# One tile or three for the column pieces of w_in

## The chip, the cores and the metric

The kernel runs on one core of a Trainium2 chip, in one launch. The metric is the time of an execution on the device in microseconds (us); lower is better. Five engines of the core matter: TensorE (PE; its weight loads are listed apart as PEld), VectorE (DVE), ScalarE (ACT), GpSimd (POOL) and SyncE (SP). Each works through its own list of instructions in order and waits on semaphores for what other engines or transfers (DMAs) must have done first. SP issues the loads of q, k, v and f_logit and the stores of the output; POOL issues the loads of the two weight matrices, among its other work.

## The reference

Two computations stand one behind the other: a recurrence over the sequence with a gate per element, and a two-layer feed-forward block on its output.

```python
B, H, S, D = q.shape                       # 4, 8, 768, 48
f = 1.0 / (1.0 + np.exp(-f_logit))
for t in range(S):
    state = f[:, :, t, :, None] * state + np.einsum('bhd,bhe->bhde', k[:, :, t], v[:, :, t])
    y[:, :, t] = np.einsum('bhd,bhde->bhe', q[:, :, t], state)
...
x = np.ascontiguousarray(y.transpose(0, 2, 1, 3)).reshape(B * S, H * D)     # 3072 x 384
h = x @ w_in                               # w_in: 384 x 2048
g = np.maximum(0.01 * h, h)
return (g @ w_out).astype(np.float32)      # w_out: 2048 x 384
```

## The kernel before

**Chunks and pairs.** The sequence is cut into 6 chunks of 128 steps. Inside a chunk the recurrence is done with matmuls on all 128 steps at once; between chunks a state is carried. The 4 batch rows go two by two, so there are 12 pairs j of (chunk, half of the batch); in a pair, a = 0 or 1 names the batch row. One (j, a) is a unit of 128 tokens.

**The order is written out by hand.** A long string `order` lists steps such as `uu_0_0_1`, and a loop at the end of the function records them one by one. Each engine runs its share in this order. The first number is j, the second as a rule a. The steps that matter here:

- `Lf`, `Lk`, `Lq`, `Lv` (line 98): SP loads 192 KB of one input for one unit. Each input has six buffers.
- `gate` (lines 136 and 137, ACT), `cs` (142 and 145, PE), `dec` (152 to 156, ACT): the gate's logarithm, its running sum by a matmul with a triangle, and the factors from it. `k` (161) and `q` (167) scale k and q, on DVE for early pairs and on POOL for later ones; `v` (174 and 175, POOL) casts v into two layouts.
- `tk`, `tq` (188, PE) and `ck`, `cq` (191, DVE): transposes. `sc` (207, PE): scores of a unit into tile pw; `mk` (212, DVE): the mask; `mx` (240, PE): the mix of values into py; `xt` (246, DVE): py becomes xT, the transposed tokens that the feed-forward block reads. `pt` (251, PE), `sf` (256 and 257, DVE), `sb` (261 and 264, POOL): the state.
- `uu_j_a_g` (line 289, PE): a quarter g of the up-projection of one unit, 12 matmuls: four blocks ff = 4g to 4g + 3 of 128 of the 2048 columns, three steps kk of 128 of the 384 rows. `pu` (294, ACT): the leaky ReLU of that quarter. `up` (276) and `pr` (282) are the same for both units of later pairs, two blocks at a time. Tile pm has two buffers, so PE fills one while ACT empties the other.
- `dn_j_a_quarter` (299, PE): four matmuls of the down-projection; `ob` (304, DVE) takes the result out of PSUM, `st` (312, SP) stores it. The last unit has its own steps, `dp`, `op` and `sp` (321, 327, 332).
- `W_piece_...` (function `weights`): POOL issues the transfer of a piece of the weights, which come as float32 and are written as bfloat16. Before the first, a copy of one number makes POOL wait for the load that the step names (line 108). Pieces 0 to 2 are columns 0 to 511, 512 to 1023 and 1024 to 2047 of w_in (line 111); pieces 3 to 6 are quarters of w_out (line 115).
- `H_piece` (function `hold`, line 128): SP issues a transfer of four numbers out of a piece of the weights, and so waits until that piece has landed; the loads behind it on SP wait with it. The order uses `H_4` alone, the second quarter of w_out.

**The weights on the chip.** w_in lies in one tile, `w_in_b` of shape [128, 3, 2048]: in each of the 128 partitions three rows kk of 2048 numbers one behind the other. Which columns make up a block ff is told by `columns(ff)`: with c, a = divmod(ff, 4), every fourth column from 512c + a on, within the 512 columns of group c. So quarter g of a unit reads the columns 512g to 512g + 511: quarter 0 those of the first piece, quarter 1 those of the second, quarters 2 and 3 those of the third.

**Around the pieces, in the order.** `W_0`, `W_1`, `W_2` and `W_3` are recorded among the steps of pairs 0 and 1. On PE, what reads w_in first is `uu_0_0_0` and `uu_0_1_0`; then come `sc_1_1`, `mx_1_0`, `uu_0_0_1`, `uu_0_1_1`, `pt_1_0`, `uu_1_0_0`, `mx_1_1`, `uu_1_0_1`, `uu_0_0_2`, `uu_0_1_2`, `pt_1_1`, `uu_0_1_3`, `uu_0_0_3`, and the first step of the down-projection, `dn_0_0_0`. The waits are not written by hand: the framework derives them from which parts of which tiles an instruction reads or writes.

Of the kernel before, what the change touches and what calls it, by code (L numbers as in the profile page):

```python
# [10 lines left out]
BF16 = mybir.dt.bfloat16  # L11
# [4 lines left out]
def kernel(  # L16
# [10 lines left out]
    nc = tc.nc  # L27
# [6 lines left out]
    KD, FF = moe_w_in.shape  # L34
    NK, NF = KD // 128, FF // 128
# [8 lines left out]
    const = ctx.enter_context(tc.tile_pool(name="const", bufs=1))  # L44
# [29 lines left out]
    nc.gpsimd.memset(ones_col, 1.0)  # L74
    gate_w = const.tile([1, 8], FP32, tag="gate_w")

    w_in_b = const.tile([128, NK, FF], BF16, tag="w_in")
    w_out_b = const.tile([128, NF, KD], BF16, tag="w_out")

    for t in v2s:  # L80
# [4 lines left out]
    st = {j: {} for j in range(NP)}  # L85
# [7 lines left out]
    def raw(j, name):  # L93
        return once(j, name + "_raw", lambda: inp.tile([128, 2, H, D], FP32, name=f"{name}_raw", tag=f"{name}_raw"))
# [4 lines left out]
                          in_=srcs[name][2 * h + a, :, c * C:(c + 1) * C, :].rearrange("h t d -> t h d"))  # L99

    seen = set()
    w_in_cols = ((0, FF // 4), (FF // 4, FF // 2), (FF // 2, FF))

    def weights(piece, x, j, a):

        if (x, j, a) not in seen:
            seen.add((x, j, a))
            nc.gpsimd.tensor_copy(out=gate_w[:, 0:1], in_=raw(j, "fkqv"[x])[0:1, a, H - 1, D - 1:D])
        if piece < 3:
            lo, hi = w_in_cols[piece]  # L110
            nc.gpsimd.dma_start(out=w_in_b[:, :, lo:hi], in_=moe_w_in[:, lo:hi].rearrange("(k p) n -> p k n", p=128))  # L111
        else:
            n = NF // 4
            part = piece - 3
            nc.gpsimd.dma_start(
                out=w_out_b[:, part * n:(part + 1) * n, :],
                in_=moe_w_out[part * n * 128:(part + 1) * n * 128, :].rearrange("(p a) n -> p a n", a=n))
# [3 lines left out]
    def hold(piece):  # L121

        if piece < 3:
            hi = w_in_cols[piece][1]
            src = w_in_b[0:1, NK - 1, hi - 4:hi]
        else:
            src = w_out_b[0:1, (piece - 2) * (NF // 4) - 1, 0:4]
        nc.sync.dma_start(out=gate_s[:, 0:4], in_=src)
# [134 lines left out]
            rows = slice(64 * i, 64 * i + 64)  # L263
            nc.gpsimd.tensor_copy(out=sb[rows, a, :, i * D:i * D + D], in_=sf[rows, a])  # L264

    def columns(ff):

        c, a = divmod(ff, 4)
        return slice(512 * c + a, 512 * c + 512, 4)

    def up(j, g):
        pm = st[j]["pm", g] = ps_m.tile([128, 2, 256], FP32, name="pm", tag="pm")
        for i in range(2):
            ff = 2 * g + i
            for kk in range(NK):
                nc.tensor.matmul(pm[:, i, :], w_in_b[:, kk, columns(ff)],  # L276
                                 st[j]["xT"][:, kk].rearrange("t a s -> t (a s)"),
                                 start=(kk == 0), stop=(kk == NK - 1))

# [4 lines left out]
    def up_unit(j, a, g):  # L284
        pm = st[j]["pu", a, g] = ps_m.tile([128, 4, 128], FP32, name="pm", tag="pm")
        for i in range(4):
            ff = 4 * g + i
            for kk in range(NK):
                nc.tensor.matmul(pm[:, i, :], w_in_b[:, kk, columns(ff)], st[j]["xT"][:, kk, a, :],  # L289
                                 start=(kk == 0), stop=(kk == NK - 1))  # L290

    def relu_unit(j, a, g):
# [36 lines left out]
    def store_part(j, a, i):  # L329
# [8 lines left out]
        "xk": lambda j: turn_dma(j, "k"), "xq": lambda j: turn_dma(j, "q"),  # L338
        "sc": score, "mk": mask, "mx": mix, "xt": x_out, "pt": state, "sf": state_add, "sb": state_end,
        "up": up, "pr": relu, "uu": up_unit, "pu": relu_unit, "W": weights, "H": hold, "dn": down, "ob": out_copy, "st": store,  # L340
        "dp": down_part, "op": out_part, "sp": store_part,
        "Lf": lambda j, a: load(j, "f", a), "Lk": lambda j, a: load(j, "k", a),
# [96 lines left out]
```

## Time and profile before

| | |
|---|---|
| three runs | 194.6, 195.93 and 196.33 us, median 195.93 |
| the profiled execution | 195.9 us in all, span of the profile 194.1 us |
| PE busy | 173.9 us, 90% of the span |
| PEld, DVE, ACT, POOL busy | 71%, 50%, 51%, 39% |
| granted TensorE clock | 1.00 of full speed |
| transfers | 27.10 MB, 140 GB/s in the mean |
| w_in | two transfers of 384 KB and one of 768 KB, issued by POOL from 14.2 us on |

Times in the profile are counted from the start of the span. A row of the timeline gives the start, the length, the engine, line and operation, the tiles (out<-in), how many instructions are taken together, and in brackets for how long the engine had been idle before and what ended that. The chain of waits goes back from the last instruction to what released each step, and so holds only work that set the end. SPq and POOLq are the issuing of transfers; a transfer's time to landing counts from its issue. PE's matmuls overlap, so a group's length divided by its count is the pace, while the mean length of one is longer than that.

### The profile page before, as it was taken

The numbers are of one execution on the slowest core, as the hardware profiler recorded it, in microseconds if no ns is written. First come the engines' busy times: TensorE is split into PE (matmuls) and PEld (weight loads), VectorE is DVE, ScalarE is ACT, GpSimd is POOL, SyncE is SP. The second block draws the span as 40 slices with busy tenths as digits, with TensorE's granted clock in tenths as the row PEclk, the third lists the DMA queues.
The fourth block names the chain that finished last, engine by engine and source line by source line (L and its number), as shares of the span: only waits on it lengthen the run. The fifth ranks groups of instructions, "written<-read, shape, count | busy, mean of one in ns | idle before, by whom it ended". The sixth has DMA issues, their size and how long they took to land.

```text
span 194.1 us, 5638 instructions
## 1 busy us (share of the span) xinstructions
PE 173.9 (90%) x2360; PEld 138.1 (71%) x2360; DVE 97.5 (50%) x212; ACT 98.8 (51%) x201; POOL 75.1 (39%) x138
## 2 busy tenths in 40 slices
PE   0476229999999999999999999999999999999994
PEld 0343128977687888878888778877868888888663
DVE  2398503107688856966347737509737574200131
ACT  4544004726654788544976376974233544644200
POOL 8237060030439089401999373099653040000000
PEclk9999999999999999999999999999999999999999
DMA  6999999934999889979798989991001000021122
GB/s 121 210 197 169 204 195 206 173 75 111 200 213 206 191 160 230 178 171 211 162 239 195 210 184 212 194 244 57 26 19 57 28 5 3 3 78 44 41 81 81
DMA packets 106113, 27.10 MB, mean 140 GB/s; under 512 B 100456, under 2 KB 105192, under 8 KB 106088
## 3 DMA queue, kind: packets, MB, share of 16 engines
q1 hardware_dynamic: 104312, 23.60, 57.1%
q0 software_dynamic: 1776, 3.15, 9.0%
q8 instruction: 18, 0.29, 0.6%
q14 instruction: 7, 0.06, 0.1%
HBM read 25.17 MB, written 4.72 MB: 154 GB/s over the span
## 4 chain that ended last, share of the span: by engine, by line
PE 84%; DMA 8%; SPq 5%; POOL 1%; issue 0%; DVE 0%
PE po L299 31%; PE pm L276 22%; PE pm L289 12%; DMA w_in_b<-in_moe_w_in_dram 6%; PE py L240 5%; PE tp L188 5%; SPq L98 5%; PE pw L207 3%; PE cs L142 2%; DMA v_raw<-in_v_dram 2%; PE pt L251 2%; PE po L321 1%; POOL w_in_b L111 1%; PE cs L145 1%; DVE osb L327 0%
## 5 line engine op out<-in xcount | busy, mean ns | idle before, releaser
L299 PE MATMUL po<-w_out_b,gT 128*128 128x384 bf16 x368 | 71.4, 326 | 0.0
L282 ACT ACTIVATE gT<-pm 128x512 bf16<-128x512 f32 x64 | 37.9, 598 | 38.2 <-PE pm L276 37.5
L276 PE MATMUL pm<-xT,w_in_b 128*128 128x256 bf16 x384 | 51.5, 273 | 0.0
L299 PEld LDWEIGHTS <-gT 128*128 128x128 bf16 x368 | 34.1, 98 | 16.2 <-issue 0.2
L276 PEld LDWEIGHTS <-w_in_b 128*128 128x128 bf16 x384 | 40.7, 114 | 4.6
L212 DVE TENSOR_TENSOR wm<-pw,ut 128x512 bf16<-128x512 f32 x48 | 30.5, 683 | 14.8 <-PE pw L207 14.6
L289 PE MATMUL pm<-xT,w_in_b 128*128 128x128 bf16 x384 | 27.2, 225 | 7.0 <-DMA w_in_b<-in_moe_w_in_dram 7.0
L304 DVE COPY osb<-po 128x384 f32<-128x384 f32 x23 | 12.6, 553 | 37.8 <-PE po L299 36.5
L294 ACT ACTIVATE gT<-pm 128x512 bf16<-128x512 f32 x32 | 18.7, 596 | 24.8 <-PE pm L289 24.5
L289 PEld LDWEIGHTS <-w_in_b 128*128 128x128 bf16 x384 | 24.5, 116 | 9.3 <-issue 6.8
L167 POOL TENSOR_TENSOR qh<-q_raw,a_t 128x384 bf16<-128x384 f32 (+1 forms) x12 | 15.7, 1308 | 23.3 <-ACT a_end L156 15.8
L174 POOL CAST v_b<-v_raw 128x384 bf16<-128x384 f32 (+1 forms) x18 | 11.3, 625 | 33.1 <-DMA v_raw<-in_v_dram 32.3
L246 DVE CAST xT<-py 128x384 bf16<-128x384 f32 x24 | 12.7, 553 | 16.9 <-PE py L240 16.8
L152 ACT ACTIVATE em_t<-cs 128x384 bf16<-128x384 f32 x24 | 11.7, 488 | 12.3 <-PE cs L145 8.7
L261 POOL TENSOR_TENSOR sf<-sf,a_end 128x192 f32<-128x192 f32 x20 | 10.5, 523 | 18.9 <-DVE sf L257 18.6
L264 POOL CAST sb<-sf 64x192 bf16<-64x192 f32 x40 | 14.2, 354 | 5.2 <-PE py L240 2.8
L142 PE MATMUL cs<-lf,ut 128*128 128x384 bf16 x24 | 8.5, 352 | 7.5 <-ACT lf L137 7.5
L136 ACT ACTIVATE e_t<-f_raw 128x384 f32<-128x384 f32 (+1 forms) x18 | 11.3, 629 | 6.4 <-DMA f_raw<-in_f_logit_dram 6.4
L191 DVE COPY kT<-tp 128x512 bf16<-128x512 bf16 x24 | 10.1, 421 | 8.2 <-PE tp L188 8.0
L188 PE MATMUL tp<-ident,qh 128*128 128x128 bf16 x96 | 10.2, 234 | 2.3 <-DVE qh L167 2.2
L153 ACT ACTIVATE a_t<-cs 128x384 bf16<-128x384 f32 x24 | 11.7, 489 | 0.0
L137 ACT ACTIVATE lf<-e_t 128x384 bf16<-128x384 f32 (+1 forms) x18 | 11.4, 631 | 0.6
(46 smaller groups left out, 172.2 us busy)
## 6 DMA issues: line engine op xcount, KB each, us to landing
f_raw<-in_f_logit_dram SPq DMA_DIRECT2D x24, 192.0 KB, 3.8
k_raw<-in_k_dram SPq DMA_DIRECT2D x24, 192.0 KB, 3.8
q_raw<-in_q_dram SPq DMA_DIRECT2D x24, 192.0 KB, 4.0
v_raw<-in_v_dram SPq DMA_DIRECT2D x24, 192.0 KB, 3.9
out_dram<-osb SPq DMA_DIRECT2D x17, 192.0 KB, 2.9
w_out_b<-in_moe_w_out_dram POOLq DMA_DIRECT2D x4, 384.0 KB, 7.5
out_dram<-osb SPq DMA_DIRECT2D x12, 96.0 KB, 1.7
w_in_b<-in_moe_w_in_dram POOLq DMA_DIRECT2D x2, 384.0 KB, 8.1
```

The costliest lines, as they stand in the source:

```text
L142: nc.tensor.matmul(t[:, 0:H * D], ut, lf[:, a, :, 0:D], start=True, stop=True)
L167: eng.tensor_mul(qhs[j % NR][:, a, :, 0:D], raw(j, "q")[:, a], st[j]["a"][:, a].rearrange("t a (h d) -> t a h d", d=D))
L188: nc.tensor.transpose(tp[:, p, :], scaled(j, x)[:, a, 2 * p:2 * p + 2, :], ident)
L212: nc.vector.tensor_mul(wm, st[j].pop(("pw", a, i)), ut[:, None, :].to_broadcast([128, P2, 128]))
L246: nc.vector.tensor_copy(out=xT[:, :, a, :], in_=st[j].pop(("py", a))[:, 0:NK, :])
L264: nc.gpsimd.tensor_copy(out=sb[rows, a, :, i * D:i * D + D], in_=sf[rows, a])
L276: nc.tensor.matmul(pm[:, i, :], w_in_b[:, kk, columns(ff)], st[j]["xT"][:, kk].rearrange("t a s -> t (a s)"), start=(kk == 0), stop=(kk == ...
L282: nc.scalar.activation(gT[:, 2 * g:2 * g + 2, :], st[j].pop(("pm", g)), AF.Prelu, alpha=0.01)
L289: nc.tensor.matmul(pm[:, i, :], w_in_b[:, kk, columns(ff)], st[j]["xT"][:, kk, a, :], start=(kk == 0), stop=(kk == NK - 1))
L294: nc.scalar.activation(gT[:, 4 * g:4 * g + 4, 128 * a:128 * a + 128], st[j].pop(("pu", a, g)), AF.Prelu, alpha=0.01)
L299: nc.tensor.matmul(po, st[j]["g"][:, ff, 128 * a:128 * a + 128], w_out_b[:, ff, :], start=(ff == 0), stop=(ff == NF - 1))
L304: nc.vector.tensor_copy(out=osb, in_=st[j].pop(("po", a)))
```

## The change

Each of the three column pieces becomes a tile of its own, [128, 3, 512], [128, 3, 512] and [128, 3, 1024]; together they take the same room. `weights` writes a whole tile; `columns(ff)` becomes `w_in(kk, ff)`, which picks the tile that holds the group of 512 columns and counts the columns from that tile's start. The text of the order, the transfers' bytes and the holds stay as they are; `hold` for pieces 0 to 2, which the order does not use, reads four other numbers of the piece.

```diff
-    w_in_b = const.tile([128, NK, FF], BF16, tag="w_in")
+    w_in_cols = ((0, FF // 4), (FF // 4, FF // 2), (FF // 2, FF))
+    w_in_b = [const.tile([128, NK, hi - lo], BF16, name="w_in_b", tag=f"w_in{lo}") for lo, hi in w_in_cols]
...
-            nc.gpsimd.dma_start(out=w_in_b[:, :, lo:hi], in_=moe_w_in[:, lo:hi].rearrange("(k p) n -> p k n", p=128))
+            nc.gpsimd.dma_start(out=w_in_b[piece], in_=moe_w_in[:, lo:hi].rearrange("(k p) n -> p k n", p=128))
...
-            hi = w_in_cols[piece][1]
-            src = w_in_b[0:1, NK - 1, hi - 4:hi]
+            src = w_in_b[piece][0:1, NK - 1, 0:4]
...
-    def columns(ff):
+    def w_in(kk, ff):
 
         c, a = divmod(ff, 4)
-        return slice(512 * c + a, 512 * c + 512, 4)
+        piece = [hi > 512 * c for lo, hi in w_in_cols].index(True)
+        lo = 512 * c - w_in_cols[piece][0]
+        return w_in_b[piece][:, kk, lo + a:lo + 512:4]
...
-                nc.tensor.matmul(pm[:, i, :], w_in_b[:, kk, columns(ff)],
+                nc.tensor.matmul(pm[:, i, :], w_in(kk, ff),
...
-                nc.tensor.matmul(pm[:, i, :], w_in_b[:, kk, columns(ff)], st[j]["xT"][:, kk, a, :],
+                nc.tensor.matmul(pm[:, i, :], w_in(kk, ff), st[j]["xT"][:, kk, a, :],
```

More of the change, by code (lines that the diff above doesn't have):

```diff
@@ L101 @@
     seen = set()
-    w_in_cols = ((0, FF // 4), (FF // 4, FF // 2), (FF // 2, FF))
     def weights(piece, x, j, a):
```

## The prediction

> **What bounds the kernel now.** I read the page first, then the chain of waits, the windows, and last the timeline where the chain leaves TensorE.
>
> ```profile
> span 194.1 us, 5638 instructions
> ...
> PE 84%; DMA 8%; SPq 5%; POOL 1%; issue 0%; DVE 0%
> PE po L299 31%; PE pm L276 22%; PE pm L289 12%; DMA w_in_b<-in_moe_w_in_dram 6%; PE py L240 5%; PE tp L188 5%; SPq L98 5%; PE pw L207 3%; PE cs L142 2%; DMA v_raw<-in_v_dram 2%; PE pt L251 2%; PE po L321 1%; POOL w_in_b L111 1%; PE cs L145 1%; DVE osb L327 0%
> ...
> L289 PE MATMUL pm<-xT,w_in_b 128*128 128x128 bf16 x384 | 27.2, 225 | 7.0 <-DMA w_in_b<-in_moe_w_in_dram 7.0
> ```
>
> The chain that ended last is 84% PE work. Of the rest one item, the transfer of w_in, holds 6% of the span, and line 289 is the only large PE group with real idle time before it: 7.0 us, waiting for that transfer. The windows and the list of PE's waits from 28 us on say the same by stage (columns of a window: its length, then PE, PEld, DVE, ACT, POOL busy with counts, granted clock, DMA share, GB/s):
>
> ```profile
> 21.30:28.00 6.70, 0.29 (x1) 0.11 (x1) 0.65 (x2) 0.00 (x0) 3.50 (x8) 1.00 1.17 207
> 28.04:180.00 151.96, 151.94 (x2159) 123.67 (x2159) 80.02 (x169) 88.51 (x178) 61.20 (x103) 1.00 0.65 138
> ```
>
> ```profile
> PE pm L289 <- DMA w_in_b<-in_moe_w_in_dram: 6.4, 1, 6.4
> ```
>
> From 21.30 to 28.00 PE runs one matmul. From 28.04 to 180 it is busy for 151.94 of 151.96 us, and the wait of 6.4 us, which ends at 28.04, is the only one that the list has. A microsecond taken out before 28 us is therefore worth a microsecond at the end, provided everything that PE reads later can come earlier too.
>
> The hole itself, first in the timeline, then in the account of the tile w_in_b:
>
> ```profile
> 21.30 0.30 PE L289 MATMUL pm<-xT,w_in_b 128*128 128x128 bf16 x1 [0.54 <-DMA w_in_b<-in_moe_w_in_dram]
> 28.04 2.62 PE L289 MATMUL pm<-xT,w_in_b 128*128 128x128 bf16 x23 [6.44 <-DMA w_in_b<-in_moe_w_in_dram]
> ```
>
> ```profile
> L111 POOL DMA_DIRECT2D w_in_b<-in_moe_w_in_dram x3: 772/786/946, 14.2 to 15.9; - x3
> ...
> DMA to landing us min/median/max: 7.0/9.2/12.0
> ```
>
> An issue holds POOL for 0.77 to 0.95 us. The first piece lands at 14.2 + 7.0 = 21.2; the second, issued 0.77 to 0.95 later, at 24.2 to 24.4 with its 9.2; the third at 15.94 + 11.96 = 27.90 (first row of the chain below). The first two units of up-projection, uu_0_0_0 and uu_0_1_0 (24 matmuls), read columns 0 to 511 alone, and those are the first piece. Matmul 1 (kk = 0) starts at 21.30, right after it landed. Matmul 2 (kk = 1) reads the same columns and yet starts at 28.04, right after the third piece, of which it reads nothing. In the one tile the row kk = 1 of columns 0 to 511 lies, in each partition, between the first and last element of the third piece (columns 1024 to 2047 of kk = 0 to 2): the wait is taken by the stretch from first to last element, not by what is read.
>
> **The change, part by part.** Three tiles hold the pieces, so a read of one has no stretch in common with a write of another. In the built programs PE's instructions stand in the same order; three waits on the transfers' semaphores remain three, but two move:
>
> ```
> before: 1st weight load of uu_0_0_0: piece 1;  2nd weight load: pieces 2 and 3
> after:  1st weight load of uu_0_0_0: piece 1;  1st of uu_0_0_1: piece 2;  1st of uu_0_0_2: piece 3
> ```
>
> ACT, VectorE, POOL and SP keep order and waits. The same rows of w_in are moved with the same bytes by the same three issues; the hold that is used (H_4) reads w_out_b and is untouched. Weight loads still read with a step of 4 elements, at another offset: nothing added, 0 us.
>
> The gain is what PE can do before it meets the two moved waits. The chain of waits, 14 to 44 us, gives that work as it runs back to back:
>
> ```profile
> 15.94 11.96 DMA w_in_b<-in_moe_w_in_dram
> 27.90 0.14 issue
> 28.04 2.62 PE pm L289 x23
> 30.65 0.54 PE pw L207 x8
> 31.20 0.52 PE py L240 x16
> 31.71 1.46 PE pm L289 x24
> 33.17 0.17 PE pt L251 x4
> 33.34 0.68 PE pm L289 x12
> 34.02 0.34 PE py L240 x16
> 34.36 1.46 PE pm L289 x24
> ...
> 38.18 0.65 PE po L299 x4
> ```
>
> Matmuls of the first group take 2.62/23 = 0.114 us each, so matmul 2 can start at 21.30 + 0.11 = 21.41 in place of 28.04: everything is 6.63 us earlier if nothing else is late. Checked one by one: pw (score of pair 1) goes from 30.65 to 24.02; uu_0_0_1, first reader of piece 2, from 31.71 to 25.08, 0.7 after its landing; uu_0_0_2, first reader of piece 3, is the second half of the row at 34.36, 34.36 + 0.73 = 35.09, and goes to 28.46, 0.56 after 27.90. Neither moved wait holds PE. What lies beside it: the activations of these units follow PE on ACT, which does nothing in the window from 21.30 to 28.00 (0.00 busy); the casts of v that the second py reads end at 24.81, and that py goes from 34.02 to 27.39:
>
> ```profile
> 24.52 0.29 POOL L175 CAST v<-v_raw 128x128 bf16<-128x128 f32 x1
> ```
>
> Next late could be w_out, the loads of pair 2, and then the stream of loads. Rows of the account of line 115, of SyncE's queue (three places), of ACT (two), and the page's row of the f_raw loads with its median time to landing:
>
> ```profile
> L115 POOL DMA_DIRECT2D w_out_b<-in_moe_w_out_dram x4: 536/564/604, 16.7 to 27.2; - x4
> ...
> DMA to landing us min/median/max: 5.5/7.5/13.0
> ```
>
> ```profile
> 31.56 0.73 SPq L128 DMA_DIRECT2D gate_s<-w_out_b  x1
> 32.34 0.40 SPq L98 DMA_DIRECT2D f_raw<-in_f_logit_dram  x1
> ```
>
> ```profile
> 37.64 0.78 SPq L98 DMA_DIRECT2D k_raw<-in_k_dram  x1
> 45.37 0.36 SPq L312 DMA_DIRECT2D out_dram<-osb  x1
> ```
>
> ```profile
> 60.16 0.72 SPq L98 DMA_DIRECT2D f_raw<-in_f_logit_dram  x1
> 62.63 0.36 SPq L312 DMA_DIRECT2D out_dram<-osb  x1
> ```
>
> ```profile
> 43.80 0.53 ACT L136 ACTIVATE e_t<-f_raw 128x384 f32<-128x384 f32 x1
> ```
>
> ```profile
> 111.42 0.84 ACT L136 ACTIVATE e_t<-f_raw 128x768 f32<-128x768 f32 x1 [0.78 <-DMA f_raw<-in_f_logit_dram]
> ```
>
> ```profile
> f_raw<-in_f_logit_dram SPq DMA_DIRECT2D x24, 192.0 KB, 3.8
> ```
>
> - w_out: the first part lands at 16.7 + 13.0 = 29.7; dn_0_0_0 goes from 38.18 to 31.55. The second lands by 31.56, when H_4 passes; the last, issued at 27.2, by 36.7 even at 9.5 us (15.0 for the middle two, less 5.5), and dn_0_0_3 reads it: between dn_0_0_0 and it the order has 24 matmuls of line 299 (0.65/4 each) and 36 of line 289 (1.46/24), 6.1 us, so it goes to 31.55 + 6.1 = 37.6. No wait.
> - Pair 2: f_raw lands at 32.34 + 3.8 = 36.1; its gate goes from 43.80 to 37.17. These six loads start behind H_4 and do not move, and their cover shrinks from 7.7 to 1.0 us: no wait, but here the profile would show one first.
> - The stream: SyncE stands from 38.42 to 45.37 at the store of pair 0, whose data come from PE. It goes to 38.74, when the six loads are issued. The queue, empty from about 41.4 (37.64 + 3.8) to 45.4 now, is then never empty, so the stream comes forward by some 4.0 us at once, not 6.63. It catches up at 60.88 (60.16 + 0.72), where SyncE now stands 1.75 us at another store of PE's results. That makes 5.75 of 6.63; the 0.9 left falls on gates such as the one at 111.42, where ACT now waits 0.78 and PE loses nothing. I take 0 for it.
>
> Sum: -6.63 us. Bounds: a gain over 7.19 is excluded, since uu_0_0_2 cannot start before 27.90 (35.09 - 27.90); below, 5.75 if the 0.9 lands on PE.
> The profiled execution took 195.9 in all (span 194.1 and 1.8 around it), as the median 195.93 does; three runs lie from 194.6 to 196.33. Predicted: 195.9 - 6.6 = **189.3 us**, span 187.5.
>
> The rate of the first group bears on it: 0.114 us a matmul from 28.04, 1.46/24 = 0.061 from 31.71 of the same shape, with a granted clock of 1.00 throughout. I take the slow stretch of 3.67 us as moving along unchanged.
> The Trainium skill (TensorE: Matmul & The Clock Gate, Part 1: The HAM clock gate) says that the array falls to half rate after an idle window of about 3.4 us and needs about that much sustained work to leave it, with a phase that varies; the trace agrees in both rates. By it the stretch could end earlier (gain up to the 7.19 of the third piece) or last a window longer, the second rival below.
>
> **Rivals.**
> - The stream of loads does not catch up: gain 4.0 to 4.8 (with the 0.78 of ACT's wait as the tolerance shown), 191.1 to 191.9. For it: the gate at 111.42, which has no slack left. Against: the 1.75 us stand.
> - Slow matmuls last longer: PE enters the work at 21.41 out of sparse work. A second stretch of 3.67 us at 0.114 in place of 0.061 costs 3.67 x (1 - 0.061/0.114) = 1.7: gain 4.9, 191.0. Against: before 28.04 PE was idler still.
> The same page of the Trainium skill gives the phase of the window as the reason why such a stretch varies.
> - Nothing moves (the wait is for something else): 195.9. Against: the waits in the built programs.
> - Slower: the pieces land later in tiles of another row length. The point from which it decides is 35.09, piece 3's need before. At the slowest rate per byte shown (13.0 us for 384 KB of w_out) the 768 KB take 26.0, land at 41.9, and uu_0_0_2 is 6.9 late: 202.8. For: the same 384 KB took 5.5 to 13.0 here. Against: same bytes, issues and neighbours.
>
> **How the numbers follow.** About 1% (2 us) is what a measurement of this kernel can tell from no change. Forecast 0.77, loads 0.09, slow matmuls 0.06, nothing 0.04, slower 0.04. The first three are faster by more than 1%: 0.92; same 0.04; slower 0.04. The forecast's own range is 188.7 to 190.2 (gains 7.19 and 5.75). The range goes up to 191.9 for the first two rivals, and down to 187.9, half the runs' spread (0.87) below 188.7.
>
> **What would show it.** Right: in the timeline line 289 runs all 24 matmuls from 21.3; PE's idle time before line 289 falls from 7.0 to about 0.5; in the chain the third piece (11.96 us) gives way to the first (7.0); the first store is issued near 38.7; the windows after 28 us stay full. Wrong: a wait for w_in_b of more than 0.5 us near 25 or 28 us, a gate of pair 2 that waits for f_raw, PE idle between 60 and 130 us, or a slow stretch past 25.1.

## The result, and the profile after

The changed kernel takes 189.08 us in the median of five executions (188.21 to 190.06), against 196.07 us before (five executions, 194.60 to 196.37). The ratio is 0.9656, with a 95% interval of 0.9605 to 0.9707: between 5.7 and 7.7 us of 196.07. The ratios leave out executions more than 1.5% above the fastest of the same kernel, here and below: two of six in each kernel with fillers. The profiled execution took 189.08 us with a span of 187.3, against 195.9 and 194.1: 6.8 us less. Line numbers have moved a little: the up-projection by units is now line 290 (289 before), the down-projection 300 (299), the stores 313 (312), the loads 99 (98).

The page, and then the windows (length; PE, PEld, DVE, ACT, POOL busy with counts; granted clock; DMA share; GB/s):

```profile
span 187.3 us, 5637 instructions
...
PE po L300 32%; PE pm L277 23%; PE pm L290 13%; PE py L239 5%; PE tp L187 5%; SPq L99 5%; DMA w_in_b<-in_moe_w_in_dram 3%; PE pw L206 3%; DMA v_raw<-in_v_dram 2%; PE cs L141 2%; PE pt L250 2%; PE po L322 1%; PE cs L144 1%; DVE osb L328 0%; POOL gate_w L108 0%
...
L290 PE MATMUL pm<-xT,w_in_b 128*128 128x128 bf16 x384 | 27.6, 228 | 0.3 <-DMA w_in_b<-in_moe_w_in_dram 0.3
```

```profile
21.30:28.00 6.70, 6.70 (x109) 5.92 (x107) 2.33 (x5) 2.98 (x5) 3.14 (x8) 1.00 1.12 214
28.04:180.00 151.96, 151.94 (x2092) 121.85 (x2090) 79.53 (x169) 86.55 (x175) 61.29 (x103) 1.00 0.65 138
```

The same 6.70 us in which PE ran one matmul are now full, with 109. Line 290 waits 0.3 us where line 289 waited 7.0, and the transfer of w_in has gone from 6% of the chain to 3%. PE stays full behind it. The chain of waits through the start:

```profile
14.02 6.52 DMA w_in_b<-in_moe_w_in_dram
20.54 0.04 issue
20.58 2.75 PE pm L290 x24
23.33 0.54 PE pw L206 x8
23.87 0.55 PE py L239 x16
24.42 1.96 PE pm L290 x24
26.38 0.17 PE pt L250 x4
26.55 0.68 PE pm L290 x12
27.23 0.34 PE py L239 x16
27.57 1.46 PE pm L290 x24
...
31.39 0.65 PE po L300 x4
```

The transfer in it is now the first piece (6.52 us, from 14.02), where it was the third (11.96, from 15.94). All 24 matmuls of the first two units run in one go. The first step of the down-projection starts at 31.39 in place of 38.18, 6.79 us earlier, and the span ends 6.8 us earlier: what is won here arrives at the end whole.

### The profile page after: what moved, and what is told of

Same layout as the page of the kernel before. It is cut to its first block, busy times and chain, and to the rows that moved or that the text cites. A ratio compares the mean times of both kernels' runs of the same rounds, so it can differ in the third digit from the quotient of the medians.

```text
span 187.3 us, 5637 instructions
## 1 busy us (share of the span) xinstructions
PE 174.2 (93%) x2360; PEld 138.6 (74%) x2360; DVE 97.6 (52%) x212; ACT 98.8 (53%) x201; POOL 75.0 (40%) x138
## 4 chain that ended last, share of the span: by engine, by line
PE 88%; DMA 5%; SPq 5%; issue 0%; DVE 0%; POOL 0%
PE po L300 32%; PE pm L277 23%; PE pm L290 13%; PE py L239 5%; PE tp L187 5%; SPq L99 5%; DMA w_in_b<-in_moe_w_in_dram 3%; PE pw L206 3%; DMA v_raw<-in_v_dram 2%; PE cs L141 2%; PE pt L250 2%; PE po L322 1%; PE cs L144 1%; DVE osb L328 0%; POOL gate_w L108 0%
## 5 line engine op out<-in xcount | busy, mean ns | idle before, releaser
L166 POOL TENSOR_TENSOR qh<-q_raw,a_t 128x384 bf16<-128x384 f32 (+1 forms) x12 | 15.7, 1306 | 23.6 <-ACT a_end L155 16.3
L173 POOL CAST v_b<-v_raw 128x384 bf16<-128x384 f32 (+1 forms) x18 | 11.3, 625 | 25.7 <-DMA v_raw<-in_v_dram 22.0
L135 ACT ACTIVATE e_t<-f_raw 128x384 f32<-128x384 f32 (+1 forms) x18 | 11.3, 630 | 4.6 <-DMA f_raw<-in_f_logit_dram 4.6
```

What stands on the lines that cost most here:

```text
L166: eng.tensor_mul(qhs[j % NR][:, a, :, 0:D], raw(j, "q")[:, a], st[j]["a"][:, a].rearrange("t a (h d) -> t a h d", d=D))
```

## The experiments

Each was compared with the kernel before, run on the same chip. Since that one's median differs by up to 1.4 us from set to set (194.72 to 196.07), the ratios are what to compare; the three tiles have 0.9656 [0.9605, 0.9707].

**One tile again, without overlap.** The pieces are three views of one tile, each without a break in a partition, at the places that the three tiles had.

```diff
-    w_in_b = [const.tile([128, NK, hi - lo], BF16, name="w_in_b", tag=f"w_in{lo}") for lo, hi in w_in_cols]
+    w_in_one = const.tile([128, NK * FF], BF16, name="w_in_b", tag="w_in")
+    w_in_b = [w_in_one[:, NK * lo:NK * hi].rearrange("p (k n) -> p k n", k=NK) for lo, hi in w_in_cols]
```

> One tile again, but each piece stands in it as one stretch without a break, at the same places as with three tiles. If the wait came from the overlap of the stretches from first to last element, PE runs line 289's work from about 21 us without a break and the time is that of three tiles, 188.2 to 190.1 us. If a read of a tile waits for all transfers into that tile, whatever the place, the wait of 6.4 us is back and the time is about 196.

188.24 us (187.49 to 189.76), ratio 0.9669 [0.9604, 0.9735]. The list of PE's waits from 20 us on has no wait of 6.4 us:

```profile
PE pm L291 <- DMA w_in_b<-in_moe_w_in_dram: 0.6, 1, 0.6
PE tp L188 <- DVE kh L161: 0.2, 1, 0.2
```

The wait that is left, 0.6 us, is that for the first piece. So the number of tiles is not what counts. The wait was taken because the pieces' stretches from first to last element overlapped.

**Pieces 2 and 3 share a tile.**

```diff
-    w_in_b = [const.tile([128, NK, hi - lo], BF16, name="w_in_b", tag=f"w_in{lo}") for lo, hi in w_in_cols]
+    w_in_first = const.tile([128, NK, FF // 4], BF16, name="w_in_b", tag="w_in0")
+    w_in_rest = const.tile([128, NK, 3 * FF // 4], BF16, name="w_in_b", tag="w_in1")
+    w_in_b = [w_in_first, w_in_rest[:, :, 0:FF // 4], w_in_rest[:, :, FF // 4:]]
```

> Piece 1 has its own tile, pieces 2 and 3 share one. By the theory of the stretches matmul 2 of uu_0_0_1 (kk = 1, from about 25 us) waits for piece 3, which lands at 27.0 to 27.9; behind it stand 3.4 us of work up to uu_0_0_2, which then starts at 30.5 to 31.4 in place of 28.3: 2.2 to 3.1 us over the three tiles, 191.3 to 192.2 us, with a wait of 2 to 3 us at about 25 in the profile. If the hole at the start is hidden by something else that is late anyway (the stream of loads), the time stays at 189.

193.2 us (191.27 to 194.04, ten executions), ratio 0.9878 [0.9837, 0.9919]. The profiled one has a span of 192.2. Its timeline of PE, and three of its windows:

```profile
23.57 0.25 PE L292 MATMUL pm<-xT,w_in_b 128*128 128x128 bf16 x1
27.20 2.64 PE L292 MATMUL pm<-xT,w_in_b 128*128 128x128 bf16 x23 [3.38 <-DMA w_in_b<-in_moe_w_in_dram]
```

```profile
20.00:26.50 6.50, 3.82 (x53) 3.21 (x51) 3.38 (x7) 1.19 (x2) 3.50 (x8) 0.98 1.15 209
27.20:33.00 5.80, 5.80 (x66) 5.41 (x67) 0.56 (x1) 1.79 (x3) 0.00 (x0) 0.50 1.01 198
33.50:40.00 6.50, 6.49 (x89) 5.44 (x87) 0.00 (x0) 3.42 (x6) 1.27 (x4) 1.00 0.83 163
```

The wait stands where the theory put it: behind matmul 1 of uu_0_0_1, until the third piece. It costs more than the 2.2 to 3.1 us expected: by the ratios 4.4 us over the three tiles (0.9878 - 0.9656, of 196), and in the profiled execution, the slowest of the ten, 4.9 in the span. PE stood still from 23.8 to 27.2, and after that the granted clock is 0.50 (0.98 over the window to 26.5 puts its fall at about 26.2, 2.4 us after the last matmul); 23 matmuls take 2.64 us (0.115 each) in place of 1.4 at the full pace. Matmul 2 comes 2.7 us later than in the three tiles (27.20 against 24.42 + 0.09), the down-projection 4.9: here the wait is paid a second time in pace, which neither theory had. Whether that is so in every execution is open: two of the ten took 193.5 and 193.7 us with a mean granted clock of 1.00.

**Pieces 1 and 2 share a tile.**

```diff
-    w_in_b = [const.tile([128, NK, hi - lo], BF16, name="w_in_b", tag=f"w_in{lo}") for lo, hi in w_in_cols]
+    w_in_half = const.tile([128, NK, FF // 2], BF16, name="w_in_b", tag="w_in0")
+    w_in_last = const.tile([128, NK, FF // 2], BF16, name="w_in_b", tag="w_in1")
+    w_in_b = [w_in_half[:, :, 0:FF // 4], w_in_half[:, :, FF // 4:], w_in_last]
```

> Pieces 1 and 2 share a tile, piece 3 has its own. Matmul 2 of uu_0_0_0 waits for piece 2, which lands 3.1 to 3.4 us after piece 1: that much over the three tiles, 192.2 to 192.5 us, and the wait stands at 21 to 24 us. If what counts is only that the large piece 3 is out of the way, 189.

191.4 us (190.42 to 192.39), ratio 0.9839 [0.9772, 0.9905], by the ratios 3.6 us over the three tiles. Timeline of PE in the profiled execution, the fastest of the four:

```profile
20.54 0.29 PE L292 MATMUL pm<-xT,w_in_b 128*128 128x128 bf16 x1
22.59 2.65 PE L292 MATMUL pm<-xT,w_in_b 128*128 128x128 bf16 x23 [1.76 <-DMA w_in_b<-in_moe_w_in_dram]
```

Matmul 2 waits, as the theory says, and for the second piece. The wait is 1.76 us and not over 3, since here the second piece landed 2.0 us after the first (22.55 against 20.5); how far the pieces land apart changes from execution to execution (3.1 us in the kernel before, 3.4 in the three tiles). With the two runs before, the place of the wait follows from which pieces share a stretch: three layouts, three places.

**The loads of pair 2 held longer,** in the three tiles and in the kernel before: SP passes when the last quarter of w_out has landed, not the second.

```diff
-    ... uu_1_0_2 H_4 Lf_2_0 ...
+    ... uu_1_0_2 H_6 Lf_2_0 ...
```

> The three tiles, but SP holds the loads of pair 2 until the last quarter of w_out has landed (about 34.5 us) and not the second (30.7): these loads come 3.8 us later. If their cover has shrunk to the 1 to 2 us that the sum gave, the gates of pair 2 wait 2.0 and 2.7 us for f_raw, ACT's work behind them is late, and the time rises by 0.5 to 2.5 us, to 189.6 to 191.6. If the loads of pair 2 still have the 7 us that they had before the change, nothing moves: 189.

> The one tile of before, with the same later hold as in the run of the three tiles with the last quarter of w_out held (loads of pair 2 some 3 to 4 us later). If the cover of these loads was 7.7 us before the change, nothing moves: 194 to 196.3 us, as before itself, and no gate of pair 2 waits for f_raw. If the loads of pair 2 were close to the bound already, 196.5 to 198.

With the three tiles 190.28 us, ratio 0.9767 [0.9714, 0.982], some 2 us more than without the edit (0.9767 - 0.9656, of 196; the two intervals just fail to meet). With the kernel before 194.74 us, ratio 0.998 [0.9955, 1.0005]: nothing. The gates of pair 2 in the timeline of ACT and PE's waits from 30 us on with the three tiles, then the first gate with the kernel before:

```profile
38.40 0.53 ACT L135 ACTIVATE e_t<-f_raw 128x384 f32<-128x384 f32 x1 [1.94 <-DMA f_raw<-in_f_logit_dram]
...
42.63 0.53 ACT L135 ACTIVATE e_t<-f_raw 128x384 f32<-128x384 f32 x1 [1.72 <-DMA f_raw<-in_f_logit_dram]
```

```profile
PE cs L141 <- ACT lf L136: 1.3, 2, 1.1
```

```profile
42.66 0.53 ACT L136 ACTIVATE e_t<-f_raw 128x384 f32<-128x384 f32 x1
```

After the change the gates wait for f_raw, and PE's running sum of pair 2 waits 1.3 us for the gates; before it the gate finds its data there (a row without brackets has no idle time before it). The cover of these loads did shrink with the change, as the sum had it. The hold passed 4.2 us later in the first kernel (34.97 against 30.72) but only 2.0 in the second (33.60 against 31.56), so the two are not the same dose. The larger one would not have changed this: in the first kernel f_raw landed at 38.4, and in the kernel before its gate starts at 42.66.

**Idle PE filled.** 72 matmuls of no use, in bursts of 5 to 24 ahead of six early steps, into a tile that nobody reads.

```diff
+    def warm(n):
+        po = ps_o.tile([128, KD], FP32, name="po", tag="po")
+        for i in range(n):
+            nc.tensor.matmul(po[:, 0:128], ident, ident, start=(i == 0), stop=(i == n - 1))
...
+    ... wm_24 cs_0_0 ... wm_13 tq_0_0 ... wm_9 cs_0_1 ... wm_8 tq_0_1 ... wm_13 cs_1_1 ... wm_5 tk_1_0 ...
```

> The three tiles, and 72 matmuls of no use in PE's idle time before 18 us. If the slow pace of the first matmuls of line 289 (0.114 us against 0.061) comes from PE having been idle for much of the time before, they run at 0.061 from the first, PE reaches its first need of piece 3 up to 1.9 us earlier, and piece 3 (landing at 26.4 to 27.1, need at 28.3) lets through 1.2 to 1.9 of it: 187.2 to 188.2 us. If the pace is set by the transfers that land at the same time, or the fillers hold up the steps behind them, 189.1 or more.

190.12 us (188.10 to 194.21, six executions), ratio 0.9698 [0.9645, 0.975]: not faster than the three tiles. The profiled execution, the fastest (188.10 us), shows that the pace can be had from the first matmul on. Timeline of PE:

```profile
20.31 1.50 PE L290 MATMUL pm<-xT,w_in_b 128*128 128x128 bf16 x24
```

The first two units take 1.50 us, not 2.75, while the transfers run as they did (DMA share 1.23 in that stretch): the pace comes from PE's own activity before, not from the transfers. But of the six executions only this one has a mean granted clock of 1.00; the others have 0.96 to 0.98.

**Piece 3 in two transfers and two tiles,** alone and with the fillers; the fourth transfer is issued right behind the third, and the quarters of w_out keep their order:

```diff
-    w_in_cols = ((0, FF // 4), (FF // 4, FF // 2), (FF // 2, FF))
+    w_in_cols = tuple((i * FF // 4, (i + 1) * FF // 4) for i in range(4))
...
-    ... gate_1_1 W_2_3_1_0 mk_0_1_1 ...
+    ... gate_1_1 W_2_3_1_0 W_7_3_1_0 mk_0_1_1 ...
```

> The three tiles with piece 3 cut into two transfers and two tiles of 512 columns. uu_0_0_2 needs the first of them alone. If piece 3 has 0.6 to 1.2 us to spare, as the sum said, nothing moves: 188.2 to 190.1 us. If piece 3 still holds PE in some executions, up to 0.6 us less in the median.

> Both: the fillers and the cut of piece 3. If the fillers alone are held by piece 3, the cut sets free what is left, and the time is 0.3 to 0.7 us below the fillers alone, 186.7 to 187.7 us. If the fillers do nothing, 189.

Alone 188.52 us (187.36 to 189.95), ratio 0.9655 [0.961, 0.97], the same as the three tiles: piece 3 did not hold PE. With the fillers 190.17 us (188.19 to 191.41), ratio 0.9749 [0.9704, 0.9794], worse than alone. Windows of the profiled execution with the fillers:

```profile
14.40:21.00 6.60, 4.82 (x59) 3.64 (x56) 5.24 (x11) 1.98 (x5) 5.63 (x10) 0.50 0.99 172
21.20:28.00 6.80, 6.47 (x132) 5.74 (x131) 3.90 (x8) 3.48 (x6) 2.64 (x6) 1.00 1.19 195
```

PE had reached the full pace, lost it again among the attention steps for a whole stretch with a granted clock of 0.50, and had it back for the up-projection (1.00 from 21.20). A stretch of 6.8 us at 0.50 takes 1.8% from the mean over 187 us, which is the 0.982 that several executions show. What decides whether the pace is lost is not shown. In the 6.8 us before the fall PE was about as busy in this execution as in the profiled one of the fillers alone, which kept its pace; first with the cut of piece 3, then the fillers alone:

```profile
7.50:14.30 6.80, 4.67 (x81) 3.31 (x80) 5.33 (x13) 3.85 (x10) 1.63 (x3) 1.00 1.02 201
```

```profile
7.50:14.30 6.80, 4.73 (x82) 3.36 (x81) 5.31 (x13) 3.84 (x10) 1.83 (x5) 1.00 1.09 215
```

So with fillers an execution can trade one slow stretch for another. They were not tuned further.

**Piece 3 issued behind the first quarter of w_out.**

```diff
-    ... gate_1_1 W_2_3_1_0 mk_0_1_1 q_1_0 cs_1_1 W_3_3_1_0 ...
+    ... gate_1_1 W_3_3_1_0 mk_0_1_1 q_1_0 cs_1_1 W_2_3_1_0 ...
```

> The three tiles, with piece 3 issued behind the first quarter of w_out instead of ahead of it. Piece 3 then lands when that quarter landed so far, 28.4 to 29.7 us, and uu_0_0_2 is due for it at about 28.3 (28.30 in the run of the three tiles). By the sum, which leaves piece 3 only 0.6 to 1.2 us to spare, PE waits 0.1 to 1.4 us there: 188.5 to 190.5 us, some 0.5 us over the three tiles, with a wait for w_in_b near 28 us. If piece 3 has more to spare than that, nothing moves and no wait shows.

188.99 us (188.88 to 189.18), ratio 0.9701 [0.9674, 0.9728]. Piece 3 landed at 28.20, and the timeline of PE shows the wait:

```profile
27.04 0.78 PE L290 MATMUL pm<-xT,w_in_b 128*128 128x128 bf16 x11
28.25 0.53 PE L290 MATMUL pm<-xT,w_in_b 128*128 128x128 bf16 x6 [0.44 <-DMA w_in_b<-in_moe_w_in_dram]
```

A delay of about a microsecond is enough for a wait, so in this execution piece 3 had no more to spare than that. In the time the 0.44 us cannot be told apart from none.

**No hold at all.**

```diff
-    ... uu_1_0_2 H_4 Lf_2_0 ...
+    ... uu_1_0_2 Lf_2_0 ...
```

> The three tiles without the hold: the six loads of pair 2 (1.2 MB) follow those of pair 1 at once, from about 15 us, and share the transfer engines with the pieces of w_in. By the slower rival's mechanism (the pieces land later) piece 3 comes when the loads let it, some 3 to 6 us later than 27, and PE waits near 25 and 28 us: 191 to 195 us, which would give back half of the gain. If the two queues do not hamper each other, the loads of pair 2 are simply early and the time is 188 to 189.

189.42 us (188.76 to 189.72), ratio 0.9708 [0.9682, 0.9735]. The expected loss of half the gain did not come. From the account of w_in_b, from that of w_out_b (line 115), and from the queue of SP:

```profile
DMA to landing us min/median/max: 7.4/9.1/12.4
```

```profile
DMA to landing us min/median/max: 12.6/13.7/15.3
```

```profile
16.69 6.84 SPq L99 DMA_DIRECT2D q_raw<-in_q_dram  x1
23.58 9.68 SPq L99 DMA_DIRECT2D v_raw<-in_v_dram  x1
```

The pieces of w_in land within 7.4 to 12.4 us, against 6.5 to 11.3 with the hold; in the other kernels with three tiles the slowest took 10.9 to 12.2, so this hardly stands out. The loads are held up: one issue takes SP 9.68 us, where 0.4 to 2 are usual. The quarters of w_out are late as well, 12.6 to 15.3 us to landing against 7.8 to 12.4 with the hold, but PE waits for none of them. More traffic on SP's queue did not make POOL's transfers late enough to give back the gain.

## Why the prediction was right, point by point

- **What bounds the kernel.** Right. One wait of PE ahead of a PE that is full to the end; taking it out moved the end by as much.
- **Why PE waited.** Right, and shown: one tile without overlap is as fast as three, and each layout with overlap puts the wait at the matmul that the overlap names.
- **The gain of 6.63 us.** 6.8 in the profiled executions, but two errors in it cancel, and that they do is luck. Matmul 2 starts at 20.58 + 0.11 = 20.69 in place of 28.04, 7.35 earlier, since the first piece landed 0.7 us earlier in this execution (20.54 against 21.25) and the sum took it as fixed. Then 0.56 is lost up to the down-projection, 0.50 of it to the next point.
- **The slow stretch moves along unchanged.** This term was off in size. The second 24 matmuls took 1.96 us where 1.46 was assumed, so the full pace came some 4.8 us after matmul 2 and not 3.7, at about 25.5 (nine of the 24 at 0.115); the slow stretch past 25.1 that the prediction named as a sign of being wrong did show. In the one tile without overlap they took 2.32. The second rival had this mechanism at 1.7 us; it came at about a third of that. The runs do not put this down to the change. In the three tiles with the later hold, which acts only behind these matmuls, the second 24 run at the full pace (1.53 us in the timeline, where the three tiles have 2.03); in the kernel before with the later hold they took 1.97. So the length differs between executions of the same work, and the profile before happened to hold a short stretch. The fillers show that the pace hangs on PE's activity before. The Trainium skill (TensorE: Matmul & The Clock Gate, Part 1: The HAM clock gate) gives a window that runs free of the kernel, so that the end of the slow stretch varies, by half a microsecond either way. The runs agree that it varies, but by more than that: counted from the first matmul of line 290, the full pace came after at most 3.4 us in the three tiles with the later hold (24.19 - 20.77) and after 4.9 in the three tiles (25.5 - 20.58).
- **The two moved waits.** Right: neither holds PE. The need of piece 3 came at 27.57 + 0.73 = 28.30, its landing at 15.7 + 11.3 = 27.0, which leaves 1.3 us and not 0.56; the kernel with piece 3 issued later waits 0.44 us, the one with piece 3 cut in two gains nothing. The upper bound of 7.19 rested on the landing of a single execution and so was no bound of the change: with piece 3 at 27.0 it would have been 8.1.
- **Pair 2.** Right that it is next in line and that it holds: f_raw is issued at 31.50 and lands some 3.9 us later, and its gate starts at 37.01, without a wait:

```profile
37.01 0.53 ACT L135 ACTIVATE e_t<-f_raw 128x384 f32<-128x384 f32 x1
```

- **The stream of loads.** Right that it costs PE nothing, wrong in the step before: the loads were to come forward by 4.0 us at once. The store of pair 0, behind which they stand, was issued 6.80 us earlier (38.57 against 45.37), and at 53.66 the load that had been issued at 60.16 was still 6.50 ahead. At the next store that was to be the place to catch up, SP stands from 53.66 + 0.82 = 54.48 to 55.83, 1.35 us, against 1.75 before:

```profile
38.57 0.36 SPq L313 DMA_DIRECT2D out_dram<-osb  x1
...
53.66 0.82 SPq L99 DMA_DIRECT2D f_raw<-in_f_logit_dram  x1
55.83 0.36 SPq L313 DMA_DIRECT2D out_dram<-osb  x1
```

So 0.4 us of its reserve was used and 1.35 is left; the sum had all of it used and 0.9 us missing. The gate that waited 0.78 us at 111.42 now waits 0.44 at 104.30, and the first rival did not come about:

```profile
104.30 0.84 ACT L135 ACTIVATE e_t<-f_raw 128x768 f32<-128x768 f32 x1 [0.44 <-DMA f_raw<-in_f_logit_dram]
```

- **The slower rival.** It did not happen (6.5 to 11.3 us to landing, 7.0 to 12.0 before), and loads in the pieces' way did not bring it about either.

None of the experiments beats the three tiles beyond its interval. What is left ahead of 20.5 us is the landing of the first piece and the attention of the first pairs.

## What to carry to other kernels

If a matmul waits for a transfer whose data it does not read, look at the layout before the schedule: parts that interleave in a partition are taken as one by this framework, and a tile for each part, or one tile in which each part is contiguous, takes the wait away. To price it, walk the chain of waits from the hole to the first instruction that does read the late part, and check what has to land for every step that moves forward; times of landing from one execution carry an error of about a microsecond, and so does the length of a slow stretch. Then ask what will be next in line: here the loads of pair 2, whose cover went from some 7 us to 1 to 2.

## What was not expected of the hardware

- A wait of 3.4 us of PE in the middle of its work can cost more than itself: in the profiled execution the granted clock then was 0.50 from 27.2 to 33.0, with 0.115 us a matmul in place of 0.061.
- The slow pace at the start does not show in the granted clock: the matmuls from 20.58 take 0.115 us each in windows with 1.00. It is the pace of one shape, group by group, that shows it.
- Without the hold both queues slow down, and unevenly: single loads took SP up to 9.68 us to issue, POOL's quarters of w_out, three of them issued 2.7 us earlier, landed within 12.6 to 15.3 us in place of 7.8 to 12.4, and its pieces of w_in, issued first, within 12.4 in place of 11.3.
